# Attention into a mixture of experts: the written order for ACT, GpSimd and SP in the first six expert tiles

## The chip, the cores and the metric

The kernel runs on one core of a Trainium2 chip. The core has five engines with instruction streams of their own: PE (TensorE, matrix products), ACT (ScalarE), DVE (VectorE), POOL (GpSimd) and SP (SyncE, which issues most of the DMAs). Each works through its own stream in order and waits where an instruction needs what another engine has not yet produced. The metric is the device time of one execution in microseconds, as the median of several runs.

## The reference

The input has 4 batches, 8 heads, 576 positions and 64 numbers in each head, all in float32. The reference is attention followed by a layer of experts:

```python
q_rot, k_rot = rotate(q), rotate(k)                    # rotary embedding
attn = softmax(q_rot @ k_rot.T / sqrt(64))             # per batch and head
x = (attn @ v).transpose(0, 2, 1, 3).reshape(4, 576, 512)
logits = x @ w_gate                                    # 8 experts
local = sigmoid(x @ w_local)
for b, s:                                              # s in order
    e = argmax(logits[b, s]) if s == 0 or local[b, s] < 0.5 else prev_e
    prev_e = e
    p = softmax(logits[b, s])
    h = maximum(x[b, s] @ w1[e], 0)                    # 512 -> 1024
    out[b, s] = p[e] * (h @ w2[e])                     # 1024 -> 512
```

A token keeps the expert of the token before it while its local gate stays at or above 0.5, so the choice of experts is a scan over the positions of a batch.

## The kernel before, in words

**Two stages.** The attention goes through 144 steps of 128 queries by 576 keys (about 0 to 296 us), and its results are written as rows of x to memory. Behind it comes a hand-written stretch that drains the last steps (the string DRAIN) and computes the routing of the last batch. From about 300 us the experts work on tiles of 128 tokens that share an expert. Every float32 factor is split into a high part in the rounded format fp32r (a CAST or a multiplication by one), and a low part, the difference (a TENSOR_TENSOR subtraction). A product is then three passes on PE.

**One expert tile t** consists of steps, each a letter in a string. The letters are read left to right and each adds its instructions to the program (lines of the kernel before in brackets):

- `f`: one of four pieces of the first product, h (L940). Behind the fourth, ACT takes the relu of it into hr (L946).
- `s`: one of four pieces of the second product of the tile before, o (L983). Behind the last, ACT scales it into os (L988) and POOL scatters it to the output (L989).
- `A`, `B`: split_w for the next tile's first weights, w_0 and w_1. `C`, `D`: split_w for the tile's own second weights, w_2 and w_3. Each of the four has two pieces of 128x1024, so pieces 0 to 7 in all. The high part is made on ACT (L882) or POOL (L884), the low one on DVE or POOL (L885), by the table SPLITS. If the next tile has the same expert, the block is jumped over by a branch (L891) on a flag that needs_of loads into a register (L863).
- `x`: turn_x for the next tile, four transposes tx on PE (L926) and the split into xs. `h`: turn_h, eight transposes th of hr (L974) and the split into hs. The high part is a cast on ACT (L303), the low one a subtraction on DVE (L307).
- `g`: the gather of the rows x of the tile after next by an indirect DMA that POOL issues (L915).

Tiles 0 to 5 have a string each (TILE_EARLY) and tiles from 6 on a common one (TILE). In tile 0 the letters are mixed with the routing's small steps, among them the exponential `ex` on ACT (L494) of `d`, which DVE writes (L491). The routine `pull` takes them one by one out of a list, at the splits. With this data tiles 1 to 3 have the expert of tile 0, tile 4 has another one, tile 5 that of tile 4, and tile 6 another.

**What sets the order.** Under `tc.manual_schedule()` every engine executes its instructions as the program wrote them. Under `tc.manual_schedule(engines=E)` only the engines in E do; where the instructions of the others stand is chosen by a scheduler, which may put them earlier or later among those of the same engine as long as the data allows it. The drain is written out for all engines. In tiles 0 to 5 the set is MAN2, PE and DVE; from tile 6 on it is all engines. The function pe_slot only marks places for the scheduler.

Of the kernel before, what the change touches and what calls it, by code (L numbers as in the profile page):

```python
# [28 lines left out]
KE = 6  # L29
# [7 lines left out]
GM = 12  # L37
PE_ = mybir.EngineType.PE
MAN1 = None
MAN2 = {mybir.EngineType.PE, mybir.EngineType.DVE}  # L40
MAN0 = {PE_}
LOAD0 = 4
ON_POOL = (125, 129, 130, 132, 134)
DRAIN = "tPststatbgttttwtguttegSuuuxXGGGSS"
MANUAL = KE
QK_LAST = 121
SPREAD_LAST = 127

# [89 lines left out]
def tile_attention_moe(ctx, tc, qk, v, tabs, turn, consts, tri, wg, wts, out):  # L138
# [265 lines left out]
    def pe_slot():  # L404
        if side["slots"] > 0:
            side["slots"] -= 1
            if side["slots"] == 0:
                next(side["parts"])
# [590 lines left out]
    def experts_phase():  # L999
        for t in range(LAST + 1):  # L1000
            first = first_product(t)
            second = second_product(t - 1) if t > 0 else iter(())
            for c in TILE_LAST if t == LAST else TILE if t >= KE else TILE_EARLY[t]:
                if c == "f":
                    k = next(first, None)
                    if k == 1:
                        if t == KE - 1:
                            finish()
                        if t < LAST:
                            needs_of(t + 1)  # L1010
                        for u in ahead(t):
                            expert_of(u)
                    if k is not None:
                        yield t
                elif c == "s":
                    if next(second, None) is not None:
                        yield t
                elif c == "x" and t < LAST:
                    turn_x(t + 1)
                elif c in "AB" and t < LAST:  # L1020
                    split_w(t + 1, "AB".index(c))
                elif c in "CD" and t > 0:
                    split_w(t, 2 + "CD".index(c))
                elif c == "h":
                    turn_h(t)
                    yield t + 1
                elif c == "T":
                    land_h(t)
                elif c == "L":
                    for u in ahead(t):  # L1030
                        for i in range(2):
                            load_pair(u, i)
                elif c == "H" and by_dma(t - 1):
                    split_landed(t - 1)
                elif c == "g":
                    if t == 0:
                        gather(4)
                        gather(5)
                    elif KE < t + 2 <= LAST:
                        gather(t + 2)  # L1040
        for _ in second_product(LAST):
            yield LAST

    def rest_phase():

        nl = nc.values_load_multi_w_load_instructions(meta[0:1, 60:61], min_val=U_LATE - 1, max_val=NLATE)[1][0]  # L1046

        def rest(t):
            with tc.If(nl > t - KE):  # L1049
                expert_of(t)  # L1050
                regs[t] = regs[t][0], None
                for k in range(8):
                    load_w(t, k)
                regs.pop(t)
                gather(t)
                turn_x(t)
                for c in range(4):
                    split_w(t, c)
                list(first_product(t))
                turn_h(t)  # L1060
                list(second_product(t))
                if t + 1 < NTILE:
                    rest(t + 1)

        if LAST + 1 < NTILE:
            rest(LAST + 1)
# [101 lines left out]
    if True:  # L1168
# [86 lines left out]
        moe = experts_phase()  # L1255
        with tc.manual_schedule(engines=MAN1):
# [32 lines left out]
                if drain[c]:  # L1289
                    drain[c].pop(0)()  # L1290
            assert not any(drain.values())
        with tc.manual_schedule(engines=MAN2):
            side["parts"] = itertools.chain.from_iterable(f() for f in route(B - 1, 1))
            for t in moe:
                pe_slot()
                if t == MANUAL:
                    break
        with tc.manual_schedule():
            for t in moe:
                pass  # L1300
        rest_phase()


# [57 lines left out]
```

## Time and profile before

| what | us |
|---|---|
| median of three runs | 546.08 |
| the three runs | 546.13, 544.13, 546.08 |
| the profiled execution | 546.83 |
| its span, first to last instruction | 545.1 |
| PE busy | 521.0 |
| DVE busy | 388.3 |
| ACT busy | 344.7 |
| POOL busy | 327.9 |

The span leaves 1.7 us of the profiled execution outside. An engine's busy time is the time in which it executes an instruction; branches, register loads and the issue of a DMA by SP are not counted. Idle time is put down to what ended it: `[0.68 <-ACT hr L946]` behind a PE row says that PE stood for 0.68 us and that ACT's instruction of line 946, which writes hr, let it go on. A row with x4 is a run of four instructions of one line.

### The profile page before, as it was taken

Reading aid. Unit: us, or ns where it says so; the run is one execution under the profiler, and the core shown is the slowest. Engines: PE = TensorE matmul, PEld = TensorE weight load, DVE = VectorE, ACT = ScalarE, POOL = GpSimd, SP = SyncE. Lnnn points to the kernel's source line nnn. Section 1 sums busy time; section 2 is a strip of 40 time slices with the busy share of each in tenths; the row PEclk is TensorE's granted clock in tenths of the full one; section 3 lists DMA queues with packets and bytes.
Section 4 is the critical chain, followed back from the end, with each engine's and each line's share of the span. In section 5 each row is a group of like instructions: output and inputs, shape, how many; then the busy total and the mean of one; then the engine's idle time right before and its main releaser. Section 6 shows DMA issues by size and latency. Waiting matters only on the chain. (4 is left out here: it accounts for less than half of the span.)

```text
span 545.1 us, 10718 instructions
## 1 busy us (share of the span) xinstructions
PE 521.0 (96%) x3281; PEld 460.4 (84%) x3281; DVE 388.3 (71%) x724; ACT 344.7 (63%) x766; POOL 327.9 (60%) x243
## 2 busy tenths in 40 slices
PE   7989999999999999999999999999999999999992
PEld 3788999999999999998888788887888887888881
DVE  6898999999999999999999935428422635421630
ACT  2799898888998999987676623353523443442440
POOL 2996989878787989887498401337511455411332
PEclk9999999999999999999999999999999999999997
DMA  8759588766877787895289305371647494737340
GB/s 264 284 125 239 166 241 241 152 200 196 245 179 213 204 223 185 209 252 132 57 157 272 86 21 174 115 272 45 227 102 246 123 342 102 247 99 232 87 167 25
DMA packets 63322, 97.37 MB, mean 179 GB/s; under 512 B 28113, under 2 KB 38353, under 8 KB 61458
## 3 DMA queue, kind: packets, MB, share of 16 engines
q1 hardware_dynamic: 60210, 86.84, 56.6%
q0 software_dynamic: 3040, 9.71, 5.5%
q8 instruction: 28, 0.46, 0.4%
q14 instruction: 44, 0.36, 0.2%
HBM read 76.98 MB, written 12.86 MB: 165 GB/s over the span
## 5 line engine op out<-in xcount | busy, mean ns | idle before, releaser
L983 PE MATMUL o<-w,hs 128*128 128x512 f32 x456 | 113.5, 398 | 0.2 <-ACT hs L964 0.2
L272 DVE TENSOR_REDUCE mn<-s 128x1 f32<-128x576 f32 x144 | 107.5, 747 | 3.6 <-PE s L267 2.2
L289 ACT ACTIVATE e<-s,mn 128x576 f32<-128x576 f32 x128 | 95.1, 743 | 18.9 <-DVE mn L272 15.4
L940 PE MATMUL h<-w,xs 128*128 128x512 f32 x444 | 106.2, 393 | 0.9 <-DVE xs L307 0.5
L267 PE MATMUL s<-m,qst 128*128 128x288 f32 x512 | 97.5, 311 | 5.4 <-ACT e L289 3.0
L307 DVE TENSOR_TENSOR ptl<-tm,pth 128x512 fp32r<-128x512 f32 x139 | 95.1, 685 | 6.4 <-ACT pth L303 4.0
L940 PEld LDWEIGHTS h<-w,xs 128*128 128x128 f32 x444 | 82.6, 188 | 19.1 <-DVE w L885 1.2
L983 PEld LDWEIGHTS o<-w,hs 128*128 128x128 f32 x456 | 83.0, 188 | 17.6 <-ACT hs L964 0.6
L989 POOL DMA_INDIRECT out_dram<-os,sidx x19 | 22.8, 1201 | 124.8 <-ACTq L891 71.4
L303 ACT CAST pth<-tm 128x512 fp32r<-128x512 f32 x139 | 80.8, 581 | 12.3 <-PE tm L325 11.2
L267 PEld LDWEIGHTS s<-m,qst 128*128 128x128 f32 x512 | 74.7, 189 | 12.1 <-ACT e L289 6.1
L325 PE MATMUL tm<-wid,e 128*128 128x128 f32 x512 | 77.1, 273 | 1.3 <-ACT e L289 0.5
L196 POOL TENSOR_TENSOR stage<-stage 128x1152 f32<-128x1152 f32 x26 | 68.9, 2665 | 14.0 <-DMA stage<-in_qk_dram 11.9
L361 PE MATMUL pv<-pth,v 128*128 128x288 f32 x256 | 76.4, 314 | 0.4 <-DVE ptl L307 0.2
L361 PE MATMUL pv<-ptl,v 128*128 128x288 f32 x256 | 76.6, 315 | 0.0
L325 PEld LDWEIGHTS tm<-wid,e 128*128 128x128 f32 x512 | 62.0, 140 | 2.2 <-DVE ptl L307 1.0
L885 DVE TENSOR_TENSOR w<-stage,w 128x1024 fp32r<-128x1024 f32 x37 | 50.7, 1403 | 15.7 <-SPq L1049 7.2
L361 PEld LDWEIGHTS pv<-pth,v 128*128 128x128 f32 x256 | 48.3, 189 | 2.8 <-DVE ptl L307 0.9
L361 PEld LDWEIGHTS pv<-ptl,v 128*128 128x128 f32 x256 | 48.4, 189 | 0.0
L307 DVE TENSOR_TENSOR xs<-tx,xs 128x512 fp32r<-128x512 f32 x19 | 13.1, 689 | 41.8 <-ACTq L891 32.2
L307 DVE TENSOR_TENSOR hs<-th,hs 128x512 fp32r<-128x512 f32 x26 | 17.5, 688 | 29.5 <-ACTq L891 17.8
L197 POOL TENSOR_TENSOR stage<-stage 128x576 f32<-128x576 f32 x26 | 36.9, 1432 | 0.2
(198 smaller groups left out, 817.3 us busy)
## 6 DMA issues: line engine op xcount, KB each, us to landing
stage<-in_wts_dram SPq DMA_DIRECT2D x84, 512.0 KB
stage<-in_qk_dram SPq DMA_DIRECT2D x13, 1152.0 KB
qst<-xq SPq DMA_DIRECT2D x56, 128.0 KB
stage<-in_v_dram SPq DMA_DIRECT2D x16, 320.0 KB
m<-xq SPq DMA_DIRECT2D x14, 288.0 KB
m<-xk SPq DMA_DIRECT2D x14, 288.0 KB
m<-xq SPq DMA_DIRECT2D x14, 256.0 KB
m<-xk SPq DMA_DIRECT2D x14, 256.0 KB
```

What stands on the lines that cost most here:

```text
L196: engine.tensor_tensor(x, x, tab[:, 2 * f:2 * f + 2], op=ALU.mult)
L197: engine.tensor_tensor(rr[:, f], x[:, 0], x[:, 1], op=ALU.add)
L267: pe.matmul(st[:, h, lo:hi], lhs, keys[:, k0:k0 + hi - lo], start=(n == 0), stop=(n == len(parts_) - 1))
L272: dve.tensor_reduce(mn, s_t[g][:, :, 0:HALF], axis=AX.XY, op=ALU.min)
L289: act.activation(dst.rearrange("p (h s) -> p h s", h=2), s_t.pop(g)[:, :, 0:HALF], AF.Exp, bias=mn, scale=-1.0, accum_out=sums[:, col:col ...
L303: act.copy(hi, src)
L307: dve.tensor_tensor(lo, src, hi.bitcast(F32), op=ALU.subtract)
L325: pe.transpose(ps[:, k], src[:, k * P:(k + 1) * P], ident)
L361: pe.matmul(pv_t[p, u], lhs.rearrange("p c d -> p (c d)"), rhs, start=(n == 0), stop=(n == 9))
L885: (pool if k in on_pool else dve).tensor_tensor(lo, src, hi.bitcast(F32), op=ALU.subtract)
L940: pe.matmul(ps[:, c], xs_t[t][:, x, k], w[y][:, c * 512:(c + 1) * 512], start=(k == 0 and n == 0), stop=(k == 3 and n == 2))
L983: pe.matmul(ps, hs_t[t][:, x, k], w[y][:, (k % 2) * 512:(k % 2 + 1) * 512], start=(k == 0 and n == 0), stop=(k == 7 and n == 2))
```

## The change

The first six expert tiles are taken under `tc.manual_schedule()`, as the later ones are, so that ACT, POOL and SP have the written order too. The two loops become one, and pe_slot is called for the same tiles.

```diff
-MAN2 = {mybir.EngineType.PE, mybir.EngineType.DVE}
-MANUAL = KE
...
-        with tc.manual_schedule(engines=MAN2):
+        with tc.manual_schedule():
             side["parts"] = itertools.chain.from_iterable(f() for f in route(B - 1, 1))
             for t in moe:
-                pe_slot()
-                if t == MANUAL:
-                    break
-        with tc.manual_schedule():
-            for t in moe:
-                pass
+                if t <= KE:
+                    pe_slot()
         rest_phase()
```

KE is 6. The instructions of PE, DVE and SP keep their sequence, but for one DVE instruction of late attention that shifts by three places; those of ACT and POOL change theirs. In the listings below a name is a tile of the program with a running number, and the changed kernel's line numbers are two lower than those of before (L882 there is L884 here).

The first place is ACT at tile 0, around the last weight casts ahead of hr_0. This is the order before:

```order
L882 CAST w_2_5147<-stage_94 128x1024 x2
L882 CAST w_3_5154<-stage_7_4948 128x1024
L882 CAST w_0_5189<-stage_94 128x1024 x2
L946 ACTIVATE hr_0_5221<-h_0_5164 128x1024
L494 ACTIVATE ex_34_5195<-d_33_5193 128x40
L303 CAST xs_1_5223<-tx_1_5224 128x512
L303 CAST hs_0_5249<-th_0_0_5250 128x512
L303 CAST hs_0_5249<-th_0_1_5257 128x512
```

And this is the same place on ACT in the changed kernel:

```order
L880 CAST w_2_5147<-stage_94 128x1024 x2
L880 CAST w_3_5154<-stage_7_4948 128x1024
L492 ACTIVATE ex_34_5195<-d_33_5193 128x40
L880 CAST w_0_5189<-stage_94 128x1024 x2
L944 ACTIVATE hr_0_5221<-h_0_5164 128x1024
L301 CAST xs_1_5223<-tx_1_5224 128x512
L889 COMPARE_AND_BRANCH
L880 CAST w_1_5073<-stage_94 128x1024
L889 UNCONDITIONAL_BRANCH x2
L301 CAST hs_0_5249<-th_0_0_5250 128x512
L301 CAST hs_0_5249<-th_0_1_5257 128x512
```

The exponential moved from behind hr_0 to ahead of the two casts of w_0, and the casts of hs_0 moved behind a block that a branch jumps over.

The second place is POOL from the scatter of tile 3 to that of tile 4, where w_2 and w_3 are tile 4's and w_0 and w_1 tile 6's (tile 5 has the expert of tile 4, and its blocks are jumped over elsewhere). Before, with the two gathers x_6 and x_7 standing together further up:

```order
L989 DMA out_0_dram<-os_3_5857,sidx_110 2304x512
L891 COMPARE_AND_BRANCH
L885 TENSOR_TENSOR w_2_5147<-stage_94,w_2_5147 128x1024
L891 UNCONDITIONAL_BRANCH x2
L891 COMPARE_AND_BRANCH
L884 TENSOR_SCALAR w_3_5154<-stage_7_4948 128x1024
L885 TENSOR_TENSOR w_3_5154<-stage_94,w_3_5154 128x1024
L891 UNCONDITIONAL_BRANCH x2
```

The same rows of POOL in the changed kernel:

```order
L987 DMA out_0_dram<-os_3_5857,sidx_110 2304x512
L889 COMPARE_AND_BRANCH
L883 TENSOR_TENSOR w_2_5147<-stage_94,w_2_5147 128x1024
L889 UNCONDITIONAL_BRANCH x2
L889 COMPARE_AND_BRANCH
L883 TENSOR_TENSOR w_3_5154<-stage_94,w_3_5154 128x1024
L882 TENSOR_SCALAR w_3_5154<-stage_7_4948 128x1024
L889 UNCONDITIONAL_BRANCH x2
```

In w_3 the subtraction of piece 6 now stands ahead of the copy of piece 7.

The third place is the gather of x_7 on POOL, which before stands behind that of x_6:

```order
L915 DMA x_6_5659<-rows_d_103,gidx_109 128x513
L915 DMA x_7_5989<-rows_d_103,gidx_109 128x513
L891 COMPARE_AND_BRANCH
L884 TENSOR_SCALAR w_1_5073<-stage_94 128x1024
L891 UNCONDITIONAL_BRANCH x2
L989 DMA out_0_dram<-os_2_5734,sidx_110 2304x512
```

In the changed kernel it stands much later, behind the copies of w_0 and w_1:

```order
L882 TENSOR_SCALAR w_0_5189<-stage_94 128x1024 x2
L889 UNCONDITIONAL_BRANCH x2
L889 COMPARE_AND_BRANCH
L882 TENSOR_SCALAR w_1_5073<-stage_94 128x1024
L889 UNCONDITIONAL_BRANCH x2
L913 DMA x_7_5989<-rows_d_103,gidx_109 128x513
L987 DMA out_0_dram<-os_4_5999,sidx_110 2304x512
```

The gather passed the scatters of tiles 2 and 3 and the weight work of tiles 4 and 6, and stands just ahead of the scatter of tile 4. Besides these places, four of the five register loads of a flag on ACT (L863) leave the end of attention for tiles 0 to 4, and in tiles 1 to 5 a few casts on ACT and pieces on POOL change places with their neighbours.

## Rows read from the trace of the kernel before

**Rows 1.** Page, busy time, share of the span and instructions.
```profile
PE 521.0 (96%) x3281; PEld 460.4 (84%) x3281; DVE 388.3 (71%) x724; ACT 344.7 (63%) x766; POOL 327.9 (60%) x243
```
**Rows 2.** Busy time by stretch (us), granted clock, DMA share, GB/s.
```profile
280.00:285.00 5.00, 4.65 (x34) 4.17 (x34) 4.94 (x10) 4.28 (x11) 4.92 (x8) 1.00 0.95 251
320.00:370.00 50.00, 50.00 (x263) 41.33 (x264) 23.72 (x59) 18.90 (x26) 14.86 (x11) 1.00 0.47 159
380.00:520.00 140.00, 139.82 (x661) 115.17 (x660) 55.25 (x57) 57.35 (x84) 48.45 (x37) 1.00 0.59 182
```
**Rows 3.** Waits of PE, 285 to 400 us: total, times, longest.
```profile
PE th L974 <- ACT hr L946: 0.7, 1, 0.7
```
**Rows 4.** Timeline of ACT, tile 0: start, duration, instructions [idle before].
```profile
301.43 4.84 ACT L882 CAST w<-stage 128x1024 fp32r<-128x1024 f32 x5
307.35 1.02 ACT L946 ACTIVATE hr<-h 128x1024 f32<-128x1024 f32 x1 [1.08 <-PE h L940]
308.27 0.23 ACT L494 ACTIVATE ex<-d 128x40 f32<-128x40 f32 x1
308.40 0.58 ACT L303 CAST xs<-tx 128x512 fp32r<-128x512 f32 x1
```
**Rows 5.** Timeline of DVE, tile 0.
```profile
307.40 0.20 DVE L491 TENSOR_TENSOR d<-lg_all,mx 128x40 f32<-128x40 f32 x1
...
307.98 2.35 DVE L885 TENSOR_TENSOR w<-stage,w 128x1024 fp32r<-128x1024 f32 x2
310.25 0.69 DVE L307 TENSOR_TENSOR xs<-tx,xs 128x512 fp32r<-128x512 f32 x1
```
**Rows 6.** Timeline of PE, tile 0.
```profile
308.43 1.09 PE L974 MATMUL th<-wid,hr 128*128 128x128 f32 x8 [0.68 <-ACT hr L946]
309.27 1.17 PE L940 MATMUL h<-w,xs 128*128 128x512 f32 x4
310.99 0.73 PE L940 MATMUL h<-w,xs 128*128 128x512 f32 x2 [0.54 <-DVE xs L307]
```
**Rows 7.** Timeline of POOL, tiles 4 to 6.
```profile
366.72 1.05 POOL L884 TENSOR_SCALAR w<-stage 128x1024 fp32r<-128x1024 f32 x1
367.74 2.39 POOL L885 TENSOR_TENSOR w<-stage,w 128x1024 fp32r<-128x1024 f32 x1
370.11 5.00 POOL L884 TENSOR_SCALAR w<-stage 128x1024 fp32r<-128x1024 f32 x3
376.07 1.07 POOL L989 DMA_INDIRECT out_dram<-os,sidx  x1 [0.95 <-POOLq L891]
```
**Rows 8.** Timeline of DVE, tiles 4 to 6.
```profile
367.80 3.42 DVE L885 TENSOR_TENSOR w<-stage,w 128x1024 fp32r<-128x1024 f32 x1 [3.31 <-POOL w L884]
...
372.16 6.30 DVE L885 TENSOR_TENSOR w<-stage,w 128x1024 fp32r<-128x1024 f32 x4 [0.34 <-POOL w L884]
```
**Rows 9.** Timeline of PE, tiles 4 to 6.
```profile
367.27 5.69 PE L983 MATMUL o<-w,hs 128*128 128x512 f32 x24
...
376.24 3.98 PE L940 MATMUL h<-w,xs 128*128 128x512 f32 x16 [0.34 <-DVE w L885]
380.05 0.60 PE L926 MATMUL tx<-wid,x 128*128 128x128 f32 x4
```
**Rows 10.** Groups by line: instructions, idle before, releasers.
```profile
L884 POOL TENSOR_SCALAR w<-stage 128x1024 fp32r<-128x1024 f32 x17 | 21.9, 1294 | 18.0 <-PE o L983 12.0 <-DMA stage<-in_wts_dram 4.3 <-PE h L940 0.9
```
**Rows 11.** Line 915, gathers: ns least, median, most; us to landing.
```profile
L915 POOL DMA_INDIRECT x<-rows_d,gidx x19: 998/1136/2054, 293.0 to 496.2; - x19
...
DMA to landing us min/median/max: 3.7/5.3/8.3
```
**Rows 12.** Line 863 on ACT, 270 to 300 us: first and last start.
```profile
L863 ACTq TENSOR_LOAD <-meta x5: 275/284/466, 276.8 to 285.4; - x5
...
L863 ACTq SEQ_ASSERT  x5: 18/18/25, 277.5 to 285.9; - x5
```

## The prediction, made before the changed kernel ran

> **What bounds the kernel now.** I read the page's busy shares first: PE is busy 96% of the span [rows 1]. A share is an average, so the second view was the table of busy time by stretch [rows 2]. [...] So the expert tiles have no idle PE time in which a delay could vanish: whatever the change makes PE wait around tile 0 stays in the end time, unless it swallows one of the waits that PE still has. The list of what PE waits for between 285 and 400 us comes third; its longest entry is 0.7 us, for hr of tile 0 [rows 3]. The last view was the order in time of each engine around tile 0 (301 to 312 us) and around tile 4 (363 to 381 us) [rows 4 to 9].
>
> In the attention stage the bound is another: from 280 to 285 us DVE is busy 4.94 of 5 us, ACT 4.28 and PE 4.65 [rows 2].
>
> **The change part by part.** PE, DVE and SP keep their sequences. ACT and POOL change in four places.
>
> *Tile 0, the exponential on ACT.* Now, ex is taken after hr_0. In the written order it stands before the two casts of w_0, and ACT must do it there. Before, the five casts run from 301.43 for 4.84 us, 0.97 each, so the third ends at 301.43 + 3 x 0.97 = 304.34 [rows 4]. The exponential reads d, which DVE writes at 307.40 + 0.20 = 307.60 [rows 5]. ACT stands from 304.34 to 307.60, does ex (0.23) until 307.85, and the two casts until 307.85 + 2 x 0.97 = 309.8. The relu hr_0, which started at 307.35 and ended at 308.37, then runs from 309.8 to 310.8 [rows 4]. Behind it, PE's transposes th start 0.06 us after hr ends, as they do now (308.37 to 308.43): 310.85 for 308.43, 2.4 us late [rows 4, 6].
>
> Not all of it stays. After th PE does four matmuls of tile 1 and then stands 0.54 us until 310.99 for the low half of xs [rows 6]. The four matmuls would start at 310.85 + 0.84 (from 308.43 to 309.27) = 311.7; they last 4 x 0.24 us (the rate is 3.98 us for 16 [rows 9]), and the fifth can start at 312.65. The low half of xs is done before that: the cast xs follows hr at about 310.8 and takes 0.58 [rows 4], DVE then takes 0.69 [rows 5], 312.1. DVE's two subtractions of w_0 in front of it (2.35 for both [rows 5]) follow the casts that end at 308.85 and 309.8, and are through at 311.0. So the wait of 0.54 is gone and the fifth matmul moves from 310.99 to 312.65: 1.65 us, of which I keep 1.6. Everything behind on PE moves by that.
>
> The bounds: nothing is left if DVE had d at 304.3 (no row says so), and 2.4 us if the low half of xs is late as well.
>
> *Tile 4, the order of two weight pieces on POOL.* Now POOL copies piece 7 (366.72, 1.05 us) and then subtracts piece 6 (367.74, 2.39 us) [rows 7]; in the written order the subtraction comes first. Either way POOL is through with both at 370.1. What changes is when DVE may subtract piece 7: it needs the copy, which is there at 367.77 now and at 370.15 then. But DVE's subtraction, started at 367.80, lasted 3.42 us, to 371.22 [rows 8], where two of the same kind on tile 0 took 2.35 [rows 5], 1.18 each; it came through about 1.1 us after POOL's subtraction ended at 370.13. So most of its head start is worth nothing now. From 370.15 it ends at 371.3 if it goes at once, and at 372.4 if it first stands behind one POOL copy (1.05). The next POOL copies start at that moment, so I take 372.4.
>
> The second product of tile 4 reads that piece in its last six matmuls, of 24 in 5.69 us, so from 367.27 + 18 x 0.237 = 371.5 [rows 9]; they would wait 0.9. PE stands 0.34 us at 376.24 for a subtraction of w [rows 9], which comes out of the same shared queue of POOL copies and DVE subtractions. The copy that went ahead does not come later, so that chain ends as it did, and the 0.9 us replaces the 0.34 and lets the rest be absorbed by work that is ready: the net is between 0 and 0.6, and I take 0.1, since PE at 376.24 is set by the end of that chain alone.
>
> [...] The trace shows 3.42 us beside a POOL subtraction and 1.18 alone [rows 5, 8]. [...]
>
> *The gather of x_7 on POOL.* Now it stands right behind that of x_6, two output scatters earlier than then. In the written order it stands behind the copies of w_0 and w_1 that end at 370.11 + 5.00 = 375.1, and ahead of the scatter that starts at 376.07 [rows 7]. With the branches between I put its start at 375.5. From issue to landing a gather takes 3.7, 5.3 or 8.3 us (least, median, most of 19) [rows 11]: it lands at 379.2, 380.8 or 383.8. PE's transposes tx_7 start at 380.05 now [rows 9]. The stall is 0, 0.75 or 3.75; I take the median, 0.75. Both sides move with what tile 0 delays, since what POOL's copies of w wait for most is PE's second product [rows 10], so the difference holds.
>
> *Register loads on ACT.* Four of the five loads of a tile's flag leave the end of attention (they stand from 276.8 to 285.4) for tiles 0 to 4. One holds ACT from 276.8 to 277.5, 0.7 us [rows 12]. The gain there lies between 0 and 4 x 0.7 = 2.8 us. I take 0, as DVE is the engine without room in that stage (4.94 of 5) [rows 2]. Their cost in tiles 0 to 4 I take as 0: ACT is busy 18.90 of 50 us there [rows 2] and PE waits for nothing; without that cover it would be 0.7 each.
>
> The rest (hs of tile 0 behind a skipped branch, xs_2 before hr_1, swaps in pieces that this routing skips) lies in ACT and POOL idle time, at 0; its bounds are a few tenths either way.
>
> The sum is 1.6 + 0.1 + 0.75 + 0 = 2.45 us. The profiled execution took 546.83 (span 545.1), so it becomes 549.3. That execution lies 0.75 above the median of the three, 546.08, and the time to be measured is compared with the median: 548.5. A measurement of this kernel can tell from no change what is over 0.5%, 2.73 us: below 543.35 or above 548.81.
>
> **The rivals.** *The gather decides.* If x_7 takes longer than the median to land, tile 6 stands at tx_7. At the worst landing the total is 1.6 + 0.1 + 3.75 = 5.45, or 551.5; halfway between median and worst it is 3.95, 550.0. For it: gathers take from 1.0 to 2.05 us on POOL itself [rows 11], and this one falls among DVE's subtractions (372.16 for 6.30) [rows 8]. Against it: half of the gathers land within the median.
>
> *DVE's subtraction keeps its 3.42 us.* From 370.15 it ends at 373.55; o_4 waits 2.05 in place of 0.9, 0.34 of which comes back: 1.75 net. The total is 1.6 + 1.75 + 0.75 = 4.1, or 550.2. For it: POOL copies follow without a pause until 375.1. Against it: the same DVE takes turns with them, four subtractions in 6.30 us [rows 8].
>
> *Not slower: the end of attention gets shorter.* The four loads give ACT back 2.8 us between 276.8 and 285.4. If PE follows ACT there, not DVE, the total is 2.45 - 2.8 = -0.35, or 545.7. It decides from 2.45 us of PE time on. For it: ACT is busy 4.28 of 5 us at 280 [rows 2]. Against it: DVE at 4.94.
>
> **How the numbers follow.** My forecast (between 1.6 and 2.9 us more; 547.7 to 549.0) gets 0.52, of which 0.44 lies within the 0.5% and 0.08 above. The late gather gets 0.25 and the long subtraction 0.11, both slower. The shorter attention gets 0.09, within 0.5% but for 0.02. The remaining 0.03, tile 0 losing less than 1.6, is within too. Together: faster 0.02, within 0.5% 0.54, slower 0.44. The range of 545.6 to 550.8 reaches down to the third rival and up to a gather 4.7 us in all; what is left out is the upper part of the first rival and scatter of the runs (2.0 us before).
>
> **What would show it.** In the changed profile: ACT standing until d is written and ex ahead of the last two casts; hr of tile 0 near 309.8; PE's wait before th near 3.1 us (0.68 + 2.4) and none for xs. On POOL a subtraction before the copy near 366 to 370; PE at o_4 waiting under 1 us; the gather of x_7 at 375 to 378, and PE's wait at tx_7. I am wrong if hr starts within 0.5 us of where it does now, if PE waits over 2 us at tx_7, or if the span up to 300 us is shorter by more than 1 us.

## The result and the profile after

The changed kernel is slower. Its median is 548.97 us (8 runs from 547.19 to 549.73) against 545.28 us of the kernel before on the same chip, a ratio of 1.0066 with a 95% interval of [1.0052, 1.0079]: 2.8 to 4.3 us more. The profiled execution took 548.37 us with a span of 546.6.

In the table of stretches (columns as in [rows 2]) the tiles behind are as full as before. What is new is the clock column between 310 and 314 us:

```profile
280.00:285.00 5.00, 4.95 (x38) 4.43 (x37) 4.94 (x11) 3.28 (x8) 4.84 (x7) 1.00 0.92 294
309.00:310.00 1.00, 0.11 (x1) 0.11 (x2) 1.00 (x2) 1.00 (x2) 0.00 (x0) 0.98 0.06 21
310.00:311.00 1.00, 1.00 (x6) 1.00 (x7) 1.00 (x3) 0.32 (x1) 0.00 (x0) 0.50 0.00 0
311.00:312.00 1.00, 1.00 (x5) 0.97 (x5) 0.47 (x3) 0.71 (x2) 0.00 (x0) 0.50 0.00 0
312.00:313.00 1.00, 1.00 (x4) 0.74 (x3) 0.83 (x2) 0.46 (x1) 0.00 (x0) 0.50 0.02 8
313.00:314.00 1.00, 1.00 (x6) 0.68 (x5) 0.19 (x1) 0.00 (x0) 0.00 (x0) 0.81 0.03 8
314.00:315.00 1.00, 1.00 (x8) 0.83 (x7) 0.53 (x1) 0.00 (x0) 0.00 (x0) 1.00 0.00 0
320.00:370.00 50.00, 50.00 (x268) 41.08 (x267) 23.05 (x59) 17.78 (x26) 11.72 (x9) 1.00 0.43 153
380.00:520.00 140.00, 140.00 (x663) 115.60 (x662) 55.94 (x59) 56.72 (x83) 49.93 (x38) 1.00 0.60 183
```

From 310 us on PE is busy without a gap, but at a granted clock of 0.50 its work takes nearly twice as long, as its rows below show (1.94 us for eight transposes in place of 1.09). The whole list of PE's waits from 285 to 400 us, against [rows 3]:

```profile
PE th L972 <- ACT hr L944: 3.0, 1, 3.0
PE pv L359 <- DVE ptl L305: 1.2, 1, 1.2
PE o L981 <- DVE w L883: 0.5, 1, 0.5
PE tm L323 <- ACT e L287: 0.5, 1, 0.5
```

There is no wait for xs, none for w ahead of h, and none at a tx, whose gather would be late. The 1.2 us of pv at the end of attention (0.2 before) are in every kernel here that has ACT's written order (1.6 in e7). The experiment e1 below has them too and is as fast as the kernel before, so they are no part of the loss. The timeline of ACT at tile 0 shows the first cause, against [rows 4]:

```profile
300.60 2.93 ACT L880 CAST w<-stage 128x1024 fp32r<-128x1024 f32 x3
306.80 0.24 ACT L492 ACTIVATE ex<-d 128x40 f32<-128x40 f32 x1 [3.27 <-DVE d L489]
306.95 1.97 ACT L880 CAST w<-stage 128x1024 fp32r<-128x1024 f32 x2
308.83 1.01 ACT L944 ACTIVATE hr<-h 128x1024 f32<-128x1024 f32 x1
```

ACT stands 3.27 us for d, and the two casts and hr follow. The timeline of PE over the same time, against [rows 6]:

```profile
306.33 0.60 PE L924 MATMUL tx<-wid,x 128*128 128x128 f32 x4
309.89 1.94 PE L972 MATMUL th<-wid,hr 128*128 128x128 f32 x8 [2.97 <-ACT hr L944]
311.49 2.50 PE L938 MATMUL h<-w,xs 128*128 128x512 f32 x6
...
318.49 0.60 PE L924 MATMUL tx<-wid,x 128*128 128x128 f32 x4
```

PE stands 2.97 us, and then the eight transposes take 1.94 us where they took 1.09. This execution reached tx of tile 1 at 306.33, 0.82 earlier than that of before (307.15), so I count from there: tx of tile 2 comes 12.16 us later (318.49 - 306.33); before, it was 9.06 (316.21 - 307.15). The change costs 3.10 us between these two rows. These are the rows of before for tx of tiles 1, 2 and 6:

```profile
307.15 0.60 PE L926 MATMUL tx<-wid,x 128*128 128x128 f32 x4
...
316.21 0.60 PE L926 MATMUL tx<-wid,x 128*128 128x128 f32 x4
...
365.44 0.60 PE L926 MATMUL tx<-wid,x 128*128 128x128 f32 x4
```

Around tile 4 the timeline of POOL, against [rows 7], has the subtraction of piece 6 (second of the two) ahead of the copy of piece 7 (first of the four), and then the gather of x_7:

```profile
366.51 4.86 POOL L883 TENSOR_TENSOR w<-stage,w 128x1024 fp32r<-128x1024 f32 x2 [1.67 <-ACT w L880]
371.34 6.03 POOL L882 TENSOR_SCALAR w<-stage 128x1024 fp32r<-128x1024 f32 x4
377.52 1.92 POOL L913 DMA_INDIRECT x<-rows_d,gidx  x1 [0.15 <-POOLq L889]
```

DVE's subtraction of piece 7 in its timeline, against [rows 8]:

```profile
372.42 2.06 DVE L883 TENSOR_TENSOR w<-stage,w 128x1024 fp32r<-128x1024 f32 x1 [5.68 <-POOL w L882]
```

And the timeline of PE from tx of tile 6 and the last part of o_4 to tx_7, against [rows 9]:

```profile
367.69 0.60 PE L924 MATMUL tx<-wid,x 128*128 128x128 f32 x4
...
374.53 1.43 PE L981 MATMUL o<-w,hs 128*128 128x512 f32 x5 [0.53 <-DVE w L883]
375.80 1.03 PE L972 MATMUL th<-wid,hr 128*128 128x128 f32 x8
376.59 5.84 PE L938 MATMUL h<-w,xs 128*128 128x512 f32 x24
382.27 0.60 PE L924 MATMUL tx<-wid,x 128*128 128x128 f32 x4
```

PE waits 0.53 us in o_4 and no longer in h. From tx of tile 6 (367.69) to tx_7 it takes 14.58 us; before it took 14.61 (365.44 to 380.05). The gather of x_7 starts at 377.52 and lands 4.2 us later, at 381.7, half a microsecond ahead of tx_7 (line 913 from 377 to 378.5 us):

```profile
DMA to landing us min/median/max: 4.2/4.2/4.2
```

### The profile page after: what moved, and what is told of

Read it like the earlier page. It is cut to its first block, busy times and chain, and to the rows that moved or that the text cites. A ratio compares the mean times of both kernels' runs of the same rounds, so it can differ in the third digit from the quotient of the medians.

```text
span 546.6 us, 10717 instructions
## 1 busy us (share of the span) xinstructions
PE 521.6 (95%) x3281; PEld 461.8 (84%) x3281; DVE 386.5 (71%) x724; ACT 344.6 (63%) x766; POOL 329.2 (60%) x243
## 5 line engine op out<-in xcount | busy, mean ns | idle before, releaser
L883 DVE TENSOR_TENSOR w<-stage,w 128x1024 fp32r<-128x1024 f32 x37 | 48.7, 1349 | 17.7 <-ACT w L880 10.8
L301 ACT CAST hs<-th 128x512 fp32r<-128x512 f32 x26 | 14.7, 589 | 38.5 <-PE th L972 38.5
```

Of the source, the lines that this page charges most:

```text
L301: act.copy(hi, src)
L883: (pool if k in on_pool else dve).tensor_tensor(lo, src, hi.bitcast(F32), op=ALU.subtract)
```

## The experiments

Two theories went into the runs. A: all of the loss is tile 0 on ACT, the late hr and the fall of the clock behind PE's pause. B: tile 0 costs the 1.6 us that I had worked out, and the rest comes from POOL's order. Two numbers are compared: the ratio to the kernel before on the same chip, and the time in one profile from tx of tile 1 to tx of tile 2, which was 9.06 us before and 12.16 in the changed kernel.

| run | ratio [95%] | tx_1 to tx_2, us | PE's wait for hr, us |
|---|---|---|---|
| e1_ex_late | 0.9996 [0.9980, 1.0012] | 9.07 | 0.68 |
| e2_act_written | 1.0044 [1.0024, 1.0065] | 12.14 | 2.97 |
| e3_pool_written | 0.9994 [0.9975, 1.0014] | 9.07 | 0.68 |
| e4_pe_filled | 1.0032 [1.0014, 1.0050] | 10.63 | filled |
| e5_changed_again | 1.0053 [1.0033, 1.0073] | 12.17 | 3.01 |
| e6_two_casts | 1.0017 [1.0003, 1.0031] | 9.25 | 1.65 |
| e7_three_casts | 1.0044 [1.0026, 1.0062] | 11.88 | 2.72 |
| e8_tile0_anew | 0.9974 [0.9961, 0.9986] | 10.29, with 12 matmuls of h_0 in it | none |

**One instruction back.** e1_ex_late is the changed kernel, with the exponential issued behind hr_0:

```diff
-            act.activation(ex, d, AF.Exp)
+            if final:
+                side["ex"] = lambda: act.activation(ex, d, AF.Exp)
+            else:
+                act.activation(ex, d, AF.Exp)
...
             act.activation(h, ps.rearrange("p c n -> p (c n)"), AF.Relu)
+            if t == 0:
+                side.pop("ex")()
```

> The changed kernel with one instruction moved: the exponential of tile 0 stands behind hr_0 on ACT again, all else as in the changed kernel (which measured +3.7 us on the kernel before). [...] Theory B (tile 0 costs only the 1.6 us of the sum, and about 2 us come from POOL's new order around the gather of x_7 and the weight pieces of tile 4): 1.5 to 2.2 us above the kernel before, 547 to 547.5.

The time is that of the kernel before (545.71 against 545.55), with the clock at 1.00 from 310 to 314 us and PE's two short waits back in its timeline:

```profile
308.61 1.10 PE L977 MATMUL th<-wid,hr 128*128 128x128 f32 x8 [0.68 <-ACT hr L947]
309.46 1.17 PE L941 MATMUL h<-w,xs 128*128 128x512 f32 x4
311.17 0.73 PE L941 MATMUL h<-w,xs 128*128 128x512 f32 x2 [0.53 <-DVE xs L305]
```

Everything else that the change moves (register loads, casts, POOL's order) together costs nothing that can be measured (-1.1 to 0.7 us). Theory B falls here.

**One engine at a time.** e2_act_written and e3_pool_written are the kernel before with one engine more in MAN2:

```diff
-MAN2 = {mybir.EngineType.PE, mybir.EngineType.DVE}
+MAN2 = {mybir.EngineType.PE, mybir.EngineType.DVE, mybir.EngineType.Activation}
```

> The kernel before with ACT added to the engines that keep the written order in tiles 0 to 5; POOL and SP are left to the scheduler. ACT's order is then that of the changed kernel. Theory A: the whole loss is here, 3.0 to 3.8 us above the kernel before, with the clock at 0.50 for about 3.4 us at tile 0. Theory B: 1.6 us above it, the rest staying with POOL.

> The kernel before with POOL added to the engines that keep the written order in tiles 0 to 5; ACT is left to the scheduler. POOL's order is then that of the changed kernel: the late gather of x_7 and the subtraction ahead of the copy in tile 4. Theory A: within 0.6 us of the kernel before. Theory B: 1.5 to 2.2 us above it, with a wait of PE at tx_7 in some executions.

ACT alone brings 1.3 to 3.5 us and POOL alone nothing (-1.4 to 0.8). In e2's timeline of PE the pause is as long as in the changed kernel:

```profile
308.96 1.09 PE L974 MATMUL th<-wid,hr 128*128 128x128 f32 x8 [2.97 <-ACT hr L946]
```

In its table of stretches the clock falls behind the pause, as there:

```profile
309.00:310.00 1.00, 1.00 (x9) 1.00 (x10) 1.00 (x2) 0.73 (x2) 0.00 (x0) 1.00 0.00 0
310.00:313.00 3.00, 3.00 (x12) 2.00 (x10) 1.47 (x4) 0.72 (x2) 0.00 (x0) 0.53 0.01 5
```

**The pause filled.** e4_pe_filled is the changed kernel with work for PE in the pause:

```diff
         for c in range(1 if by_dma(t) else 2):
             ps = ps_t.tile([P, 4, P], F32, tag="t", name=f"th_{t}_{c}")
+            if t == 0 and c == 0:
+                for k in range(30):
+                    pe.transpose(ps[:, k % 4], x_t[1][:, 0:P], ident)
```

> The changed kernel with 30 more transposes on PE, of rows of x that are there, ahead of th of tile 0 (their results are overwritten by th): PE is busy while it would stand for hr. hr is as late as in the changed kernel. Theory A: the 2.97 us of standing brought the clock down, so with work in it the clock stays at 1.00 and the time is 1.2 to 1.6 us under the changed kernel, 2.1 to 2.5 above the kernel before. Theory B, or a clock that falls for another reason: the time is that of the changed kernel, 3.7 above the kernel before.

In PE's timeline the added transposes lead to th without a wait:

```profile
307.08 0.60 PE L924 MATMUL tx<-wid,x 128*128 128x128 f32 x4
307.51 3.44 PE L973 MATMUL th<-wid,x 128*128 128x128 f32 x30
310.79 1.04 PE L975 MATMUL th<-wid,hr 128*128 128x128 f32 x8
...
317.71 0.60 PE L924 MATMUL tx<-wid,x 128*128 128x128 f32 x4
```

In ACT's timeline hr is as late as in the changed kernel, 2.50 us behind tx_1 (309.58 - 307.08):

```profile
309.58 1.01 ACT L944 ACTIVATE hr<-h 128x1024 f32<-128x1024 f32 x1
```

The stretch of PE behind it:

```profile
310.00:314.00 4.00, 4.00 (x30) 3.48 (x29) 3.46 (x6) 2.14 (x4) 0.00 (x0) 1.00 0.02 5
```

The clock stays up. From tx_1 to tx_2 it takes 10.63 us, 1.57 more than before and 1.53 less than in the changed kernel. The added transposes themselves hold th back a little: it starts 3.71 us behind tx_1 (310.79 - 307.08), and 3.56 in the changed kernel (309.89 - 306.33). Without these 0.15 us, by estimate, the late hr alone costs 1.42, where I had 1.6, and the clock the other 1.68 of the 3.10. The median, 1.9 us above the kernel before (0.8 to 2.7; 2.1 to 2.5 expected), fits the trace. Between this kernel and the changed one there is no interval from a shared chip. The median of e2, which has the pause and ran on this chip, is 1.1 us higher, but the scatter of the runs is too wide to tell that from nothing. So the split rests on the traces, and on the mean granted clocks given below.

**The changed kernel again, and hr made late in another way.** e5_changed_again repeats the changed kernel. e6 and e7 take e1 and put two or three copies on ACT ahead of hr_0 (three here):

```diff
+            if t == 0:
+                for _ in range(3):
+                    act.copy(h, w_own[0][:, 0, 0].bitcast(F32))
```

> The changed kernel as it is, on the chip and beside the kernels of this call. Theory A (the lateness of hr and the fall of the clock are all): 3.0 to 3.9 us above the kernel before, mean granted clock near 0.989 in its executions against 0.9945 before.

> The kernel with the exponential behind hr_0 (e1_ex_late), and two more copies of 128x1024 on ACT right ahead of hr_0, whose result hr_0 overwrites: hr starts about 0.95 us late, PE stands some 1.6 us before th. By the terms of the sum 0.95 - 0.53 (the wait for xs, absorbed) = 0.4 us above the kernel before, if the clock holds. Theory A adds to that only if the clock falls in this shorter pause too, 1.5 us more. A theory in which ACT's order in itself costs something: 3 us are lost only in the written order, so this one stays at the kernel before.

> As e6_two_casts with three copies: hr starts about 1.95 us late, PE stands some 2.6 us. By the terms of the sum 1.95 - 0.53 = 1.4 us above the kernel before. Theory A: PE's pause is nearly that of the changed kernel, so the clock falls to 0.50 for 3 us and more behind it, and the total is 2.5 to 3.2 us above the kernel before. If what costs is the written order in itself: no more than 0.5.

With three copies the exponential is behind hr_0, and the loss is there all the same. PE's timeline of e7 shows the pause:

```profile
310.30 1.09 PE L980 MATMUL th<-wid,hr 128*128 128x128 f32 x8 [2.72 <-ACT hr L950]
```

Its table of stretches shows the clock in the pause and behind it:

```profile
308.00:310.00 2.00, 0.00 (x0) 0.00 (x0) 2.00 (x2) 1.94 (x3) 0.00 (x0) 1.00 0.78 222
311.00:314.00 3.00, 3.00 (x12) 2.14 (x11) 1.93 (x4) 1.07 (x2) 0.00 (x0) 0.56 0.02 5
```

So it is the pause that counts in these runs, whether the exponential makes it or the copies do. In PE's timeline of e6, with two copies, it is shorter:

```profile
309.48 1.09 PE L980 MATMUL th<-wid,hr 128*128 128x128 f32 x8 [1.65 <-ACT hr L950]
```

The stretch around it has the clock at 1.00 throughout:

```profile
309.00:314.00 5.00, 4.52 (x26) 3.77 (x27) 4.51 (x7) 2.10 (x5) 0.00 (x0) 1.00 0.22 71
```

Only 0.19 us are lost there by the trace (9.25 - 9.06), under the 0.4 expected, and 0.2 to 1.7 by the runs. The wait for xs hides more than the 0.53 of its mark: from the first matmul of h_1 to the row transposes it was 2.29 us before (311.56 - 309.27) and is 1.47 in e6 (311.80 - 310.33), so 0.82 of the 0.97 us by which hr is late vanish there. What lies between pauses of 1.65 and 2.72 us was not tried. e5 took 548.39 against 544.95, with 0.55 as the clock's mean from 311 to 314 us:

```profile
311.00:314.00 3.00, 3.00 (x13) 2.46 (x11) 2.09 (x5) 1.18 (x3) 0.00 (x0) 0.55 0.02 5
```

A table of stretches shows one execution of each kernel. The mean granted clock is on record for every execution, and it tells the same: averaged over the executions it is 0.994 for the kernel before and for e1, e3, e4 and e6, and 0.990 to 0.992 for the changed kernel, e2, e5 (0.992, for 0.989 expected) and e7.

**A version that beats both.** If PE's waits are what counts, an order that has none is worth more than the scheduler's. e8_tile0_anew keeps the written order on all engines, but writes another one (the exponential stands behind hr_0 as in e1, which is not shown again):

```diff
-TILE_EARLY = ("ffAffsfxBssgCsshD", "ffAffxfsBsCsgsshD", ...
+TILE_EARLY = ("ffxAffsfBg", "fkfAffxfsBsCsgsshD", ...
...
+                elif c == "k":
+                    turn_h(t - 1)
+                    yield t
...
-SPLITS = (..., ((0, 2, 4, 5, 6), (5, 6)), ...
+SPLITS = (..., ((0, 2, 4, 5, 6, 7), (5, 6)), ...
...
+        if (t, c) == (1, 0):
+            parts()
         for k in (2 * c, 2 * c + 1):
             if k not in on_pool:
                 pull(PULL)
...
-                side["slots"] = PE_LAG
+                side["slots"] = side.pop("lag", PE_LAG)
...
+            side["lag"] = 4
```

> All engines in written order, with another order written for tile 0: the transposes of x_1 stand in the middle of h_0, the low halves of xs_1 and w_0 on DVE ahead of the routing's steps, the exponential behind hr_0, and the first six matmuls of h_1 ahead of th_0 (the row transposes two places later); besides, the copy of piece 7 in tile 4 is on ACT and not on POOL. Theory A: PE neither stands for hr (0.68 before) nor for xs (0.54), and not for weights at tile 4 (0.34 and 0.45 of slower issue): 1.2 to 2.0 us under the kernel before, near 543.7, with the clock at 1.00 through tile 0. A rival: routing's key comes 0.5 to 2 us later and PE stands for it at the row transposes, so the gain is gone: within 0.5 us of the kernel before.

The median is 543.67 us against 544.95, 0.8 to 2.1 us less. In the timeline h_1's first matmuls now run while ACT makes hr (18 in a row from 304.47, the last six of them h_1's), and th follows at once:

```profile
304.12 0.60 PE L931 MATMUL tx<-wid,x 128*128 128x128 f32 x4
304.47 4.63 PE L943 MATMUL h<-w,xs 128*128 128x512 f32 x18
308.94 1.04 PE L979 MATMUL th<-wid,hr 128*128 128x128 f32 x8
```

The rival, a wait for the routing's key, didn't come, as the stretch around the row transposes shows, and tile 4 has no wait left either (second row):

```profile
304.00:314.00 10.00, 10.00 (x53) 7.91 (x52) 8.79 (x15) 4.91 (x8) 2.39 (x2) 1.00 0.40 94
361.00:377.00 16.00, 16.00 (x77) 13.13 (x76) 11.37 (x10) 7.62 (x10) 13.62 (x7) 1.00 0.29 112
```

The kernel's two parts, tile 0 and tile 4, were not run apart.

## Why the prediction was right in direction and too small

*Tile 0 on ACT* went as worked out up to the end of the pause: hr started 2.50 us behind tx_1 (308.83 - 306.33) where it was 0.20, so 2.3 late for 2.4 foretold; PE stood 2.97 us for 3.1; the wait for xs went. The size is what failed. The step "the fifth matmul moves from 310.99 to 312.65" counted every matmul behind the pause at the rate of before. I took the granted clock of 1.00 in the table of stretches [rows 2] as given, and never asked what a pause would do to it. The term that I put at 1.6 measured 3.10: by estimate 1.42 for the lateness (from e4) and 1.68 for the clock. It was at half for some 3.4 us (from 309.96 to 313.4, by the means of the single microseconds above), and half of that is 1.7. My upper bound of 2.4 for it was too low as well.

That the pause brings the clock down rests on the runs: behind pauses of 2.72 to 3.01 us it is at 0.50 in four traces (the changed kernel, e2, e5 and e7), and with the pause filled it is at 1.00 (e4). How long a pause has to be for that was not shown; 1.65 us did not do it (e6).

*Tile 4 on POOL*: 0.1 foretold, -0.03 measured (14.58 against 14.61). The subtraction of piece 7 took 2.06 us beside POOL's copies, where it had taken 3.42 beside POOL's subtraction. So 3.42 is not its price wherever POOL is busy, and the rival that kept it is out (its net was 1.71, 2.05 - 0.34, not 1.75). That a part of the 3.42 us was a wait behind POOL, on which the 372.4 and so the 0.1 rest, was my estimate; no run shows such a wait by itself, only the durations: 1.18 us alone (half of the 2.35 in [rows 5]), 2.06 beside its copies and 3.42 beside its subtraction. PE's 0.53 us in o_4, for 0.9 foretold, took the place of the 0.34 in h.

*The gather of x_7*: 0.75 foretold, nothing measured. It landed in 4.2 us, under the median of 5.3 that I had taken; in the traces of e5 and e3 it took 4.2 and 4.3. The margin is half a microsecond, so a landing of 5.3 would still be felt, and the worst of 8.3 more; e3, with the same order on POOL, shows no loss in the median. This rival did not happen.

*Register loads*: 0 foretold; e1, which has them where the changed kernel has them, is where the kernel before is, and the changed kernel's stretch from 280 to 285 us has DVE at 4.94 of 5, as before. That tx_1 came 0.82 us earlier in the profiled execution is scatter: over the nine profiles other than e8's it lies between 305.39 and 307.33 us, and e3, whose ACT keeps its loads, has 306.52.

The sum of the measured terms is 3.10 - 0.03 = 3.07 us for 2.45 foretold. The runs say 2.8 to 4.3 here and 1.8 to 4.0 in e5, so nothing more than tile 0 is needed. The two profiled executions differ by only 1.5 us of span, because the changed one is also 0.82 us ahead at tx_1 and takes 0.7 less from tx_7 to the end. That last part is scatter too: over the same nine profiles it takes 163.7 to 165.1 us.

That the forecast came as near as it did is in part luck. The 0.75 us of the gather, which did not come, stood in for half of the 1.5 that tile 0 lacked; without it the sum would have been 1.7. The upper end of the range held the result, but it was put there for a late gather, and no rival had the clock. The forecast sat just inside the 0.5% and the result is outside.

## What to carry to other kernels

Where one engine is full and others follow it, a small instruction that waits for a third engine must not stand ahead of work that the full engine waits for: here 0.23 us of work cost 3.1 us. When a change makes TensorE stand for long (2.7 us and more here; 1.65 did not suffice), price the pause and then some work behind it at half the clock (0.50 for some 3.4 us here). Thirty spare transposes in the pause gave 1.53 us back by the traces (e4), and with work that is needed anyway in its place PE had no pause there at all (e8).

## What the runs showed of the hardware

In e2 the clock fell after the pause was over: PE resumed at 308.96, the microsecond from 309 to 310 still ran at 1.00, and the mean from 310 to 313 was 0.53. In the changed kernel PE resumed at 309.89 and the clock was at 0.50 by 310. After pauses of 2.72 to 3.01 us (the changed kernel, e2, e5 and e7) it was at 0.50 for some 3.4 us of busy work in each trace, by the means of their stretches, and then came back to 1.00; after 1.65 us (e6) it did not fall. Thirty transposes in the pause kept it at 1.00 (e4).
